# A sketched attention and an ELU block on one core: all large products in 128x64 tiles, boundary pieces last, and another order at a group's end

## The chip, the core and the metric

The kernel runs on one core of a Trainium2 chip. The core's engines run side by side, each with its own instruction queue that is worked in order: TensorE (PE) for products, VectorE (DVE), ScalarE (ACT), GpSimd (POOL), and SyncE (SP), which here only issues transfers. PE writes to PSUM, eight banks of 128 partitions x 512 fp32 numbers; the other operands lie in SBUF. The metric is the time of one execution on the device in microseconds (us), as the median of several runs.

## The reference

The first part is an attention without softmax (`q`, `k`, `v`: 4 batches, 4 heads, 1088 positions, head size 32; `S1`, `S2`: 8 x 32). The second is a two-layer block with ELU, on 4352 tokens of 128 features and 2048 hidden units.

```python
def phi(x):
    a = np.einsum('rd,bhsd->bhsr', S1, x)
    b = np.einsum('rd,bhsd->bhsr', S2, x)
    return np.einsum('bhsi,bhsj->bhsij', a, b).reshape(*x.shape[:-1], r * r)
q_p, k_p = phi(q), phi(k)
kv = np.einsum('bhsf,bhsd->bhfd', k_p, v)
z = np.sum(k_p, axis=2)
num = np.einsum('bhsf,bhfd->bhsd', q_p, kv)
den = np.einsum('bhsf,bhf->bhs', q_p, z)[..., None] + 1e-06
x = (num / den) laid out as (4352, 128)
h = x @ w_in
g = np.where(h > 0, h, np.exp(np.minimum(h, 0)) - 1)
out = g @ w_out
```

## The kernel before

**Tokens and groups.** The 4352 tokens are 68 half tiles of 64, 17 for each batch. Eight of them make a group `g` of 512 tokens; there are nine groups, 0 to 8, and the last has only 256. In groups 0 and 1 the second product is computed plainly. In groups 2 to 7 (`seven(g)`) it is computed with seven products in place of eight, from 2x2 blocks of the operands (the scheme of Winograd). Group 8 computes it with the operands swapped, so that tokens come out on partitions.

**The loop.** The hidden units are taken 256 at a time, in eight pairs `cp`. A step `n` of the list `steps` is one group and one pair. Lines 919 to 946 write the order of the work out by hand; each engine works through its own part of it in that order:
- `mm1` (line 696): two products of `W`'s columns with the group's tokens `xg`, into two PSUM banks `h` (four exist). Groups 2 to 7 do each as two halves of 64 columns (line 706, tile 128x64), the others as one (line 702, tile 128x128). The very first is `mm1_first` (line 714).
- `elu` for each of the two halves `c`: ScalarE runs a RELU of -h (line 723) and an exponential (line 725), VectorE joins them (line 731, result `gg`).
- in groups 2 to 7, `sums7` (lines 644 to 649): four sums `tt` of blocks of `gg` on GpSimd, one behind the first half, three behind the second.
- the second product of the step two before: `mm2` (line 744, 128x128), `mm2_seven` (line 664, fourteen halves of 128 moving columns in 128x64, accumulated in two banks `pa` and `pb`) or `mm2_last` (line 767, 128x128).

After a group's last step, `fin_seven` (line 669) copies three of the seven sums from `pa` on ScalarE (672), adds them up with what is in `pb` in five operations on VectorE (676 to 680), turns the result (682) and sends it out (693). `pa` and `pb` are single buffers: the next group's first products into them wait until they have been read. In a group's first step the products into `pa` come ahead of those into `pb`.

**Attention between the steps.** The dictionary `extra` puts pieces of the attention at chosen steps, in three places: behind `mm1` (`at`), between the two halves of the ELU (`mid`) and behind the second half (`late`). `KF_late` (309) projects `k`, `KA` (359) sums `kv` and, with `z_tile` (350), `z`; `turn` (lines 863 to 865) brings both to the other layout: `Z` (377), a product with 32 moving columns, and `KV` (391), two transposes on PE. `queries` (605) runs `q5` (589) of one unit around `q1` (493) of the next: `q5` for f = 0, then `q1`, then `q5` for f = 1. A unit is one group or, from group 4 on, two. Both functions use 16 tiles of 32x32, one for each head `h` and part `c` of the unit. Where a part straddles two batches, `parts(g, c)` gives two pieces, since each batch has its own operands, and the loops issue them one behind the other on the same tile. Units 2, 4 and 6 have one such part each. `q5_out` (603) and `q1_out` (505) take the results out, on ScalarE and VectorE.

Before 23.75 us the weights of the first pairs are rounded on VectorE (lines 99 to 125, `RA`, `RC`) and the first group's features are built; `Z_first` uses `Z` there too.

Of the kernel before, what the change touches and what calls it, by code (L numbers as in the profile page):

```python
# [12 lines left out]
F32 = mybir.dt.float32  # L13
# [14 lines left out]
def kernel(  # L28
# [184 lines left out]

    idle = psum.tile([P, 512], F32, name="idle", tag="o0", bufs=1)

    def keep_warm(n, cols=256):
        for i in range(n):
            nc.tensor.matmul(idle[:, :cols], some[:, :P], some[:, :cols], skip_group_check=True)  # L218
# [155 lines left out]

    def Z(b, ps, zl):

        nc.tensor.matmul(ps[:, 96:128], SXh[:], zl[:])

    def Z_out(b, ps):
        z = wzs[b] = SW[:, :, 2, :] if b == 0 else work.tile([FD, H, R], F32, name="wz", tag="wz")[:]  # L380
# [7 lines left out]

    def KV(b, ps):
        for f in range(2):  # L390
            nc.tensor.transpose(ps[:, 128 + P * f:128 + P * f + P], kvz[b][:, f].rearrange("p c s -> p (c s)"), ident[:])

    def KV_out(b, ps):
        nc.vector.tensor_copy(kvq[:, b].rearrange("p f h d -> p (f h d)"), ps[:, 128:384])
# [91 lines left out]


    def q1(g, ps, start=True):
        for c in range(4):
            for h in range(H):  # L490
                r = slice(D * h, D * h + D)
                for b, t, k, m in parts(g, c):
                    nc.tensor.matmul(ps[h][32 * c:32 * c + 32, 256 + 64 * k:256 + 64 * (k + m)],  # L493
                                     SWq[r, b].rearrange("p x r -> p (x r)"),
                                     qT[b][r, t:t + m, :].rearrange("p t s -> p (t s)"), start=start, stop=True,
                                     skip_group_check=True, tile_position=(D * h, 32 * c))
        abw[g] = ps

    def q1_out(g):
# [81 lines left out]

    def q5(g, ps, f):
        n = un[g]
        for h in range(H):
            i, o = divmod(h, heads(g))
            for c in range(4):
                r = slice(32 * c, 32 * c + 32)
                for j, (b, t, k, m) in enumerate(parts(g, c)):
                    nc.tensor.matmul(ps[c][D * h:D * h + D, 64 * k:64 * (k + m)], kvq[r, b, f, h, :],  # L589
                                     qpT[g, i][r, n * o + 2 * k:n * o + 2 * (k + m), f, :],  # L590
                                     start=(f == 0 and j == 0), stop=(f == 1),
                                     skip_group_check=True, tile_position=(32 * c, D * h))
        xps[g] = ps

    def q5_out(g, i=0):
# [28 lines left out]
    def seven(g):  # L624
        return 2 <= g < NQ - 1

    SS = const.tile([P, 4, NP, 64], F32, name="SS")
    ts, acc = {}, {}

    def weights7():  # L630
        a11, a21, a12, a22 = (W[:, :, 2 * P + 64 * i:2 * P + 64 * i + 64] for i in range(4))
# [19 lines left out]
    def mm2_seven(g, cp, first, last):  # L651
        if first:
            acc[g] = [psum.tile([P, 512], F32, name="pa", tag="o0", bufs=1),
                      psum.tile([P, 512], F32, name="pb", tag="o1", bufs=1)]
        a, b = acc[g]
        t, w = ts.pop((g, cp)), [W[:, cp, 2 * P + 64 * i:2 * P + 64 * i + 64] for i in range(4)]
        b11, b21, b22 = quarter(g, cp, 0, 0), quarter(g, cp, 1, 0), quarter(g, cp, 1, 1)
        p1, p2, p6 = (a, 0, w[0], b11), (a, 1, w[2], b21), (a, 2, SS[:, 1, cp], t[:, 1])
        p4, p5 = (b, 0, w[3], t[:, 3]), (b, 1, SS[:, 0, cp], t[:, 0])
        p7, p3 = (b, 2, SS[:, 2, cp], t[:, 2]), (b, 3, SS[:, 3, cp], b22)  # L660
        todo = [p1, p2, p6, p3, p5, p7, p4] if first else [p1, p2, p3, p5, p7, p6, p4]
        for i, (bank, col, lhs, rhs) in enumerate(todo):
            for u in range(2):
                nc.tensor.matmul(bank[64 * u:64 * u + 64, P * col:P * col + P], lhs, rhs[:, u],  # L664
                                 start=(first and i in (0, 3)), stop=last, skip_group_check=True,
                                 tile_position=(0, 64 * u))
        del gs[g, cp]

    def fin_seven(g):
        a, b = acc.pop(g)  # L670
        sa = work.tile([P, 3, P], F32, name="sa", tag="sa", bufs=1)
        nc.scalar.copy(sa[:].rearrange("p k s -> p (k s)"), a[:, :3 * P])
        pb = b[:].rearrange("p (k s) -> p k s", s=P)
        uu = work.tile([P, 3, P], F32, name="uu", tag="uu", bufs=1)
        cc = work.tile([P, 4, P], F32, name="cc", tag="cc", bufs=1)
        nc.vector.tensor_tensor(uu[:, 0], sa[:, 0], sa[:, 2], op=ADD)
        nc.vector.tensor_tensor(uu[:, 1:], _ap(uu[:, 0], [[0, 2], [1, P]]), pb[:, 1:3], op=ADD)
        nc.vector.tensor_tensor(cc[:, 2:], _ap(uu[:, 2], [[0, 2], [1, P]]), pb[:, 0:2], op=ADD)
        nc.vector.tensor_tensor(cc[:, 1], uu[:, 1], pb[:, 3], op=ADD)
        nc.vector.tensor_tensor(cc[:, 0], sa[:, 0], sa[:, 1], op=ADD)  # L680
        ob = work.tile([P, 2, 4, 2, D], F32, name="ob7", tag="ob", bufs=2)
        nc.vector.transpose(ob[:].rearrange("p h k w d -> p (h k w d)"), cc[:].rearrange("p k s -> p (k s)"))
        rows = out.rearrange("(b w y t) (e l d) -> b w e l y t d", b=B, w=2, t=NT, e=2, l=2)
        for u in range(2):
            k = 0
            while k < 4:
                bt, t = half_tile(g, 4 * u + k)
                m = min(4 - k, NT - t)
                for lo in range(2):
                    r = slice(64 * u + 32 * lo, 64 * u + 32 * lo + 32)  # L690
                    for hi in range(2):
                        for w in range(2):
                            nc.sync.dma_start(rows[bt, w, hi, lo, :, t:t + m, :], ob[r, hi, k:k + m, w, :])
                k += m

    def mm1(g, cp, cs=(0, 1)):
        n = qn[g] * P
        if 0 in cs and (g, cp) not in hs:
            hs[g, cp] = [psum.tile([P, 512], F32, name="h", tag="h", bufs=4) for c in range(2)]
        for c in cs:  # L700
            if not seven(g):
                nc.tensor.matmul(hs[g, cp][c][:, :n], W[:, cp, c * P:c * P + P], xg[g][:, :n])  # L702
                continue
            for u in range(2):
                r = slice(64 * u, 64 * u + 64)
                nc.tensor.matmul(hs[g, cp][c][r, :n], W[:, cp, c * P + 64 * u:c * P + 64 * u + 64], xg[g][:, :n],  # L706
                                 skip_group_check=True, tile_position=(0, 64 * u))

    def mm1_first():
        hs[0, 0] = [psum.tile([P, 512], F32, name="h", tag="h", bufs=4) for c in range(2)]  # L710
        for w in range(2):
            for c in range(2):
                cols = [x[:].rearrange("p (m w s) -> p w m s", w=2, s=P)[:, w] for x in (hs[0, 0][c], xg[0])]
                nc.tensor.matmul(cols[0], W[:, 0, c * P:c * P + P], cols[1], skip_group_check=True)

    def elu_a(g, cp, c, parts=(0, 1)):

# [20 lines left out]
    def mm2(g, cp, first, last):  # L738
        n = qn[g] * P
        if first:  # L740
            ops[g] = psum.tile([P, 512], F32, name="o", tag=f"o{g % 2}", bufs=1)
        gg = gs.pop((g, cp))
        for c in range(2):
            nc.tensor.matmul(ops[g][:, :n], W[:, cp, (2 + c) * P:(3 + c) * P], gg[:, c, :n],  # L744
                             start=(first and c == 0), stop=(last and c == 1))

    def fin1(g):
        n = qn[g] * P
# [11 lines left out]
    def mm2_last(cp, first, last):  # L760
        g = NQ - 1
        if first:
            ops[g] = [psum.tile([P, P], F32, name="ol", tag=t, bufs=k) for t, k in (("o0", 1), ("aux", 2))]
        gg = gs.pop((g, cp))
        for a in range(4):
            c, i = (a % 2, a // 2) if last else divmod(a, 2)
            nc.tensor.matmul(ops[g][i][:], gg[:, c, i * P:i * P + P], W[:, cp, (2 + c) * P:(3 + c) * P],  # L767
                             start=(first and c == 0), stop=(last and c == 1))

    def fin_last():  # L770
        g, n = NQ - 1, qn[NQ - 1]
# [147 lines left out]
    for n in range(2, N + 2):  # L919
# [5 lines left out]
        if n < N:  # L925
            elu(g, cp, 0)
            if seven(g):
                sums7(g, cp, 0)
            for f, *a in extra.get((n, 0), ()):
                f(*a)  # L930
            elu(g, cp, 1)
            if seven(g):
                sums7(g, cp, 1)
        for f, *a in extra.get((n, 1), ()):
            f(*a)
        g, cp = steps[n - 2]
        if g == NQ - 1:
            mm2_last(cp, cp == 0, cp == NP - 1)
        elif seven(g):
            mm2_seven(g, cp, cp == 0, cp == NP - 1)  # L940
            if cp == NP - 1:
                fin_seven(g)
        elif n > 2:
            mm2(g, cp, cp == 0, cp == NP - 1)
            if cp == NP - 1:
                fin1(g)
# [30 lines left out]
```

## Time and profile before

| what | us |
|---|---|
| median of 11 runs (272.60 to 274.82) | 274.35 |
| the profiled execution | 274.23 |
| its span | 272.4 |
| PE busy | 266.2 |
| VectorE busy | 190.8 |
| ScalarE busy | 183.4 |
| GpSimd busy | 166.2 |
| line 706, 384 records, mean 0.593 | 91.4 |
| line 744, 64 records, mean 0.604 | 30.8 |
| line 702, 92 records, mean 0.521 | 36.6 |

TensorE's granted clock is 0.999 of the full one. The times of PE's records [...] overlap: what a block costs is the distance from its start to the next block's start. Each fp32 product leaves two records, a transpose one. A timeline shows the start, the duration, the engine, the line, the operation, what is written from what, the tile (rows x columns of the array that an instruction uses), the moving shape and the number of records that were merged. A bracket at the end of a line names the idle time ahead of it and what ended it.

### The profile page before, as it was taken

What the parts mean: (1) busy time and instruction counts of PE and PEld (TensorE: products, weight loads), DVE (VectorE), ACT (ScalarE), POOL (GpSimd) and SP (SyncE); (2) the same over time, 40 slices, a digit from 0 to 9 for tenths busy, and PEclk for the clock granted to TensorE, in tenths of its full rate; (3) what the DMA queues carried; (4) which work ended last, traced back from release to release, by engine and by line L of the source; (5) the groups of instructions that cost most, each with busy time, mean ns of one, the idle gap of its engine ahead of it and who ended that gap; (6) DMA issues with size and microseconds to landing.
All of it is one profiled execution on the core that took longest, in us unless ns stands there. A gap on an engine that the chain in (4) does not pass through costs nothing.

```text
span 272.4 us, 7609 instructions
## 1 busy us (share of the span) xinstructions
PE 266.2 (98%) x3083; PEld 167.5 (61%) x3083; DVE 190.8 (70%) x350; ACT 183.4 (67%) x351; POOL 166.2 (61%) x233
## 2 busy tenths in 40 slices
PE   8899999999999999999999999999999999999994
PEld 5864444454442766666676666666766666667894
DVE  6699999997959796998648767564447444774552
ACT  2379978676564565776567677777677667777682
POOL 4500007204307985699969999989588988897200
PEclk9999999999999999999999999999999999999999
DMA  6996970011002200001100110001000200110021
GB/s 192 317 344 185 260 215 10 0 43 44 0 2 39 45 1 2 2 3 17 26 5 0 17 25 2 0 12 26 7 1 14 30 0 4 15 21 7 2 29 29
DMA packets 26418, 13.60 MB, mean 50 GB/s; under 512 B 19216, under 2 KB 24592, under 8 KB 26384
## 3 DMA queue, kind: packets, MB, share of 16 engines
q1 hardware_dynamic: 25792, 12.66, 18.8%
q8 instruction: 24, 0.39, 0.6%
q10 hardware_dynamic: 592, 0.46, 0.5%
q14 instruction: 10, 0.08, 0.1%
HBM read 10.88 MB, written 2.23 MB: 48 GB/s over the span
## 4 chain that ended last, share of the span: by engine, by line
PE 94%; DVE 4%; issue 1%; ACT 0%; DVEq 0%
PE h L706 30%; PE pb L664 16%; PE pa L664 12%; PE h L702 12%; PE o L744 11%; PE ol L767 3%; PE h L589 2%; PE idle L218 2%; PE kv L359 1%; PE abp L290 1%; PE qps L589 1%; DVE qp L536 1%; PE kfps L309 1%; PE h L493 1%; PE qps L493 1%
## 5 line engine op out<-in xcount | busy, mean ns | idle before, releaser
L731 DVE SCALAR_TENSOR_TENSOR gg<-e,h 128x512 f32<-128x512 f32 (+1 forms) x144 | 91.9, 652 | 64.7 <-ACT e L725 61.6
L723 ACT ACTIVATE e<-h 128x512 f32<-128x512 f32 (+1 forms) x144 | 81.6, 566 | 57.8 <-PE h L706 45.4
L706 PE MATMUL h<-xg,W 128*64 128x512 f32 x384 | 91.4, 593 | 0.0
L725 ACT ACTIVATE e<-e 128x512 f32<-128x512 f32 (+1 forms) x144 | 87.4, 607 | 4.6
L644 POOL TENSOR_TENSOR tt<-gg 128x256 f32<-128x256 f32 x48 | 36.3, 756 | 17.2 <-DVE gg L731 16.8
L706 PEld LDWEIGHTS h<-xg,W 128*64 128x64 f32 x384 | 27.9, 137 | 28.2 <-issue 24.9
L647 POOL TENSOR_TENSOR tt<-gg 128x256 f32<-128x256 f32 x48 | 38.3, 797 | 11.2 <-DVE gg L731 11.0
L649 POOL TENSOR_TENSOR tt<-gg,tt 128x256 f32<-128x256 f32 x48 | 37.7, 785 | 3.8
L648 POOL TENSOR_TENSOR tt<-tt,gg 128x256 f32<-128x256 f32 x48 | 37.0, 771 | 3.8
L664 PEld LDWEIGHTS pa<-gg,W 128*64 128x64 f32 x384 | 24.6, 137 | 22.4 <-issue 22.2
L702 PE MATMUL h<-xg,W 128*128 128x512 f32 (+1 forms) x92 | 36.6, 521 | 0.0
L744 PE MATMUL o<-gg,W 128*128 128x512 f32 x64 | 30.8, 604 | 0.4 <-DVE W L125 0.4
L664 PE MATMUL pa<-gg,W 128*64 128x128 f32 x384 | 30.3, 275 | 0.0
L664 PE MATMUL pb<-tt,SS 128*64 128x128 f32 x384 | 29.9, 273 | 0.0
L702 PEld LDWEIGHTS h<-xg,W 128*128 128x128 f32 x92 | 16.8, 190 | 14.9 <-issue 10.0
L664 PEld LDWEIGHTS pb<-tt,SS 128*64 128x64 f32 x384 | 23.3, 137 | 0.0
L744 PEld LDWEIGHTS o<-gg,W 128*128 128x128 f32 x64 | 11.4, 189 | 14.1 <-issue 11.9
L664 PE MATMUL pb<-gg,SS 128*64 128x128 f32 x192 | 19.5, 274 | 0.2
L664 PE MATMUL pb<-tt,W 128*64 128x128 f32 x192 | 19.4, 273 | 0.0
L664 PE MATMUL pa<-tt,SS 128*64 128x128 f32 x192 | 19.3, 273 | 0.0
L122 POOL TENSOR_TENSOR raw<-raw,tiny 128x512 f32<-128x512 f32 x1 | 1.0, 1046 | 29.3 <-DVE raw L117 29.3
L664 PEld LDWEIGHTS pb<-gg,SS 128*64 128x64 f32 x192 | 12.6, 137 | 1.0 <-issue 0.7
(141 smaller groups left out, 293.6 us busy)
## 6 DMA issues: line engine op xcount, KB each, us to landing
raw<-in_moe_w_in_dram SPq DMA_DIRECT2D x8, 256.0 KB, 5.9
raw<-in_moe_w_out_dram SPq DMA_DIRECT2D x8, 256.0 KB, 6.3
hd_k<-in_k_dram SPq DMA_DIRECT2D x3, 544.0 KB, 8.1
hd_q<-in_q_dram SPq DMA_DIRECT2D x3, 544.0 KB, 3.4
v<-in_v_dram SPq DMA_DIRECT2D x4, 288.0 KB, 6.8
out_dram<-ob SPq DMA_DIRECT2D x72, 16.0 KB, 1.5
v<-in_v_dram SPq DMA_DIRECT2D x4, 256.0 KB, 8.5
out_dram<-ob SPq DMA_DIRECT2D x16, 32.0 KB, 1.7
```

Source lines behind the costliest of these rows:

```text
L589: nc.tensor.matmul(ps[c][D * h:D * h + D, 64 * k:64 * (k + m)], kvq[r, b, f, h, :], qpT[g, i][r, n * o + 2 * k:n * o + 2 * (k + m), f, :], ...
L644: nc.gpsimd.tensor_tensor(t[:, 0], b12, b11, op=SUB)
L647: nc.gpsimd.tensor_tensor(t[:, 2], b22, b12, op=SUB)
L648: nc.gpsimd.tensor_tensor(t[:, 1], t[:, 2], b11, op=ADD)
L649: nc.gpsimd.tensor_tensor(t[:, 3], b21, t[:, 1], op=SUB)
L664: nc.tensor.matmul(bank[64 * u:64 * u + 64, P * col:P * col + P], lhs, rhs[:, u], start=(first and i in (0, 3)), stop=last, skip_group_che ...
L702: nc.tensor.matmul(hs[g, cp][c][:, :n], W[:, cp, c * P:c * P + P], xg[g][:, :n])
L706: nc.tensor.matmul(hs[g, cp][c][r, :n], W[:, cp, c * P + 64 * u:c * P + 64 * u + 64], xg[g][:, :n], skip_group_check=True, tile_position=( ...
L723: nc.scalar.activation(e, hs[g, cp][c][:, :n], RELU, scale=-1.0)
L725: nc.scalar.activation(e, e, EXP, scale=-1.0)
L731: nc.vector.scalar_tensor_tensor(gs[g, cp][:, c, :n], es[g, cp][:, c, :n], -1.0, hs[g, cp][c][:, :n], op0=ADD, op1=MAX)
L744: nc.tensor.matmul(ops[g][:, :n], W[:, cp, (2 + c) * P:(3 + c) * P], gg[:, c, :n], start=(first and c == 0), stop=(last and c == 1))
```

## The change

A new helper issues a product as two products of 64 columns each, in the two column tiles 128x64. It is used for the z product, the turning of kv (plain products with the identity in place of transposes), all first products, and the second products of groups 0, 1 and 8. In `q1` and `q5`, all first pieces are issued ahead of the second pieces. At a group's last step the order on ScalarE and VectorE is another: the products of `mm2_seven` are placed ahead of the second half's exponential in the written order (on PE they come behind the same work as before), the three products into `pa` come first, ScalarE copies only two of them between the RELU and the exponential of the second half, VectorE adds those up with the third, which it reads from PSUM, ahead of the second half of the ELU, and the rest follows behind it.

```diff
+    def halves(dst, lhs, rhs, **kw):
+        for u in range(2):
+            nc.tensor.matmul(dst[64 * u:64 * u + 64], lhs[:, 64 * u:64 * u + 64], rhs, skip_group_check=True,
+                             tile_position=(0, 64 * u), **kw)
...
-        nc.tensor.matmul(ps[:, 96:128], SXh[:], zl[:])
+        halves(ps[:, 96:128], SXh[:], zl[:])
...
-            nc.tensor.transpose(ps[:, 128 + P * f:128 + P * f + P], kvz[b][:, f].rearrange("p c s -> p (c s)"), ident[:])
+            halves(ps[:, 128 + P * f:128 + P * f + P], kvz[b][:, f].rearrange("p c s -> p (c s)"), ident[:])
...
+        todo = [(j, c, h, x) for c in range(4) for h in range(H) for j, x in enumerate(parts(g, c))]
+        for j, c, h, (b, t, k, m) in sorted(todo, key=lambda x: x[0]):
...
-                                     qT[b][r, t:t + m, :].rearrange("p t s -> p (t s)"), start=start, stop=True,
+                             qT[b][r, t:t + m, :].rearrange("p t s -> p (t s)"), start=start and j == 0, stop=True,
...
+        todo = [(j, h, c, x) for h in range(H) for c in range(4) for j, x in enumerate(parts(g, c))]
+        for j, h, c, (b, t, k, m) in sorted(todo, key=lambda x: x[0]):
...
-        todo = [p1, p2, p6, p3, p5, p7, p4] if first else [p1, p2, p3, p5, p7, p6, p4]
+        todo = [p1, p2, p6, p3, p5, p7, p4] if first or last else [p1, p2, p3, p5, p7, p6, p4]
...
+    def fin_seven_copy(g):
+        a = acc[g][0]
+        sa = sas[g] = work.tile([P, 2, P], F32, name="sa", tag="sa", bufs=1)
+        nc.scalar.copy(sa[:].rearrange("p k s -> p (k s)"), a[:, P:3 * P])
+
+    def fin_seven_a(g):
+        a, sa = acc[g][0], sas.pop(g)
...
+        nc.vector.tensor_tensor(uu[:, 0], sa[:, 1], a[:, :P], op=ADD)
+        nc.vector.tensor_tensor(cc[:, 0], sa[:, 0], a[:, :P], op=ADD)
+
+    def fin_seven_b(g):
...
         nc.vector.tensor_tensor(uu[:, 1:], _ap(uu[:, 0], [[0, 2], [1, P]]), pb[:, 1:3], op=ADD)
         nc.vector.tensor_tensor(cc[:, 2:], _ap(uu[:, 2], [[0, 2], [1, P]]), pb[:, 0:2], op=ADD)
         nc.vector.tensor_tensor(cc[:, 1], uu[:, 1], pb[:, 3], op=ADD)
-        nc.vector.tensor_tensor(cc[:, 0], sa[:, 0], sa[:, 1], op=ADD)
...
-            if not seven(g):
-                nc.tensor.matmul(hs[g, cp][c][:, :n], W[:, cp, c * P:c * P + P], xg[g][:, :n])
+            halves(hs[g, cp][c][:, :n], W[:, cp, c * P:c * P + P], xg[g][:, :n])
...
-                nc.tensor.matmul(cols[0], W[:, 0, c * P:c * P + P], cols[1], skip_group_check=True)
+                halves(cols[0], W[:, 0, c * P:c * P + P], cols[1])
...
-            nc.tensor.matmul(ops[g][:, :n], W[:, cp, (2 + c) * P:(3 + c) * P], gg[:, c, :n],
+            halves(ops[g][:, :n], W[:, cp, (2 + c) * P:(3 + c) * P], gg[:, c, :n],
...
-            nc.tensor.matmul(ops[g][i][:], gg[:, c, i * P:i * P + P], W[:, cp, (2 + c) * P:(3 + c) * P],
+            halves(ops[g][i][:], gg[:, c, i * P:i * P + P], W[:, cp, (2 + c) * P:(3 + c) * P],
...
-            elu(g, cp, 1)
+            before = steps[n - 2]
+            ends = n > 3 and seven(before[0]) and before[1] == NP - 1
+            if ends:
+                elu_a(g, cp, 1, (0,))
+                mm2_seven(*before, False, True)
+                fin_seven_copy(before[0])
+                elu_a(g, cp, 1, (1,))
+                fin_seven_a(before[0])
+                elu_d(g, cp, 1)
+            else:
+                elu(g, cp, 1)
             if seven(g):
                 sums7(g, cp, 1)
+            if ends:
+                fin_seven_b(before[0])
```

More of the change, by code (lines that the diff above doesn't have):

```diff
@@ L488, in q1 @@
     def q1(g, ps, start=True):
[L489 to L494, printed above, removed]
-                                     qT[b][r, t:t + m, :].rearrange("p t s -> p (t s)"), start=start, stop=True,
-                                     skip_group_check=True, tile_position=(D * h, 32 * c))
+        todo = [(j, c, h, x) for c in range(4) for h in range(H) for j, x in enumerate(parts(g, c))]
+        for j, c, h, (b, t, k, m) in sorted(todo, key=lambda x: x[0]):
+            r = slice(D * h, D * h + D)
+            nc.tensor.matmul(ps[h][32 * c:32 * c + 32, 256 + 64 * k:256 + 64 * (k + m)],
+                             SWq[r, b].rearrange("p x r -> p (x r)"),
+                             qT[b][r, t:t + m, :].rearrange("p t s -> p (t s)"), start=start and j == 0, stop=True,
+                             skip_group_check=True, tile_position=(D * h, 32 * c))
         abw[g] = ps
@@ L583, in q5 @@
         n = un[g]
-        for h in range(H):
+        todo = [(j, h, c, x) for h in range(H) for c in range(4) for j, x in enumerate(parts(g, c))]
+        for j, h, c, (b, t, k, m) in sorted(todo, key=lambda x: x[0]):
             i, o = divmod(h, heads(g))
[L586 to L592, printed above, removed]
+            r = slice(32 * c, 32 * c + 32)
+            nc.tensor.matmul(ps[c][D * h:D * h + D, 64 * k:64 * (k + m)], kvq[r, b, f, h, :],
+                             qpT[g, i][r, n * o + 2 * k:n * o + 2 * (k + m), f, :],
+                             start=(f == 0 and j == 0), stop=(f == 1),
+                             skip_group_check=True, tile_position=(32 * c, D * h))
         xps[g] = ps
@@ L627 @@
     SS = const.tile([P, 4, NP, 64], F32, name="SS")
-    ts, acc = {}, {}
+    ts, acc, sas = {}, {}, {}
     def weights7():
@@ L667, in mm2_seven @@
         del gs[g, cp]
[L669 to L673, printed above, removed]
+    def fin_seven_copy(g):
[4 more added lines that the diff above has]
+        a, sa = acc[g][0], sas.pop(g)
         uu = work.tile([P, 3, P], F32, name="uu", tag="uu", bufs=1)
         cc = work.tile([P, 4, P], F32, name="cc", tag="cc", bufs=1)
-        nc.vector.tensor_tensor(uu[:, 0], sa[:, 0], sa[:, 2], op=ADD)
+        sas[g] = uu, cc
+        nc.vector.tensor_tensor(uu[:, 0], sa[:, 1], a[:, :P], op=ADD)
+        nc.vector.tensor_tensor(cc[:, 0], sa[:, 0], a[:, :P], op=ADD)
+    def fin_seven_b(g):
+        b = acc.pop(g)[1]
+        uu, cc = sas.pop(g)
+        pb = b[:].rearrange("p (k s) -> p k s", s=P)
         nc.vector.tensor_tensor(uu[:, 1:], _ap(uu[:, 0], [[0, 2], [1, P]]), pb[:, 1:3], op=ADD)
@@ L700, in mm1 @@
         for c in cs:
-            if not seven(g):
[L702 to L707, printed above, removed]
+            halves(hs[g, cp][c][:, :n], W[:, cp, c * P:c * P + P], xg[g][:, :n])
     def mm1_first():
@@ L743, in mm2 @@
         for c in range(2):
-            nc.tensor.matmul(ops[g][:, :n], W[:, cp, (2 + c) * P:(3 + c) * P], gg[:, c, :n],
-                             start=(first and c == 0), stop=(last and c == 1))
+            halves(ops[g][:, :n], W[:, cp, (2 + c) * P:(3 + c) * P], gg[:, c, :n],
+                   start=(first and c == 0), stop=(last and c == 1))
     def fin1(g):
@@ L766, in mm2_last @@
             c, i = (a % 2, a // 2) if last else divmod(a, 2)
-            nc.tensor.matmul(ops[g][i][:], gg[:, c, i * P:i * P + P], W[:, cp, (2 + c) * P:(3 + c) * P],
-                             start=(first and c == 0), stop=(last and c == 1))
+            halves(ops[g][i][:], gg[:, c, i * P:i * P + P], W[:, cp, (2 + c) * P:(3 + c) * P],
+                   start=(first and c == 0), stop=(last and c == 1))
     def fin_last():
@@ L939 @@
         elif seven(g):
-            mm2_seven(g, cp, cp == 0, cp == NP - 1)
-            if cp == NP - 1:
-                fin_seven(g)
+            if cp < NP - 1:
+                mm2_seven(g, cp, cp == 0, False)
         elif n > 2:
```

## The prediction

> **What bounds the kernel now.** I read four views in this order: the chain that ended last, the timeline of TensorE (PE), the timeline of all engines at the end of one group, and the busy times by stretch. The chain, by engine:
>
> ```profile
> PE 94%; DVE 4%; issue 1%; ACT 0%; DVEq 0%
> ```
>
> PE carries nearly all of it. The DVE part lies before 23.75 us, where VectorE rounds weights and builds the first features; from 23.75 us on the end is set by the sum of PE's blocks. So I read the timeline of PE by the distance from one start to the next (the second column is modelled and runs past the next start). [...]
>
> ```profile
> 30.72 1.88 PE L702 MATMUL h<-xg,W 128*128 128x512 f32 x4
> 32.44 1.88 PE L744 MATMUL o<-gg,W 128*128 128x512 f32 x4
> ```
>
> Two products of 128x512 take 1.72 us in the 128x128 tile. In a stretch of pure 128x64 tiles (170.47, 172.00, 173.72 us) four half products of line 706 take 1.72 too, and the 14 halves of line 664 take 1.53, that is 0.2186 for a pair. Now the stretch where both kinds alternate:
>
> ```profile
> 78.19 1.94 PE L706 MATMUL h<-xg,W 128*64 128x512 f32 x8
> 80.06 0.72 PE L309 MATMUL kfps<-kT,Sxp 64*32 64x288 f32 x16
> 80.71 1.98 PE L744 MATMUL o<-gg,W 128*128 128x512 f32 x4
> 82.62 1.94 PE L706 MATMUL h<-xg,W 128*64 128x512 f32 x8
> 84.49 1.98 PE L744 MATMUL o<-gg,W 128*128 128x512 f32 x4
> ```
>
> The same work takes 1.91 (80.71 to 82.62) and 1.87. A block that enters 128x128 from another tile size costs about 0.10 more (also 58.97: 1.82), one that enters 128x64 about 0.05 (93.65: 1.58 for 1.53), and the block ahead of any change about 0.09 (37.59: 1.81 for 1.72). The last token group shows it again, with 256 moving columns:
>
> ```profile
> 250.87 1.13 PE L702 MATMUL h<-xg,W 128*128 128x256 f32 x4
> 251.93 0.66 PE L664 MATMUL pa<-gg,W 128*64 128x128 f32 x8
> ...
> 253.61 1.13 PE L702 MATMUL h<-xg,W 128*128 128x256 f32 x4
> ```
>
> 1.06 for line 702, where 258.20 to 259.07, with no change of tile, is 0.87; line 664's step is 1.68.
>
> **Part one: everything in 128x64.** Step by step, on PE's path:
> - 76.28 to 88.27, six blocks: 1.91 becomes 1.77 (still entered from 32x32 or 64x32) twice, 1.87 becomes 1.81, 1.72 and 1.81, 1.92 becomes 1.72. Gain 0.14+0.14+0.06+0.15+0.20+0.05 = 0.74.
> - Blocks of line 744 at 40.04, 58.97 and 67.21: entry at 0.05 in place of 0.10, gain 0.16.
> - 249.24 to 257.31: 1.63, 1.06, 1.68, 1.06, 1.68, 0.96 become 1.53, 0.87, 1.53, 0.87, 1.53, 0.87. Gain 0.87.
> - The eight steps of line 767: 0.89 becomes four pairs at 0.2186 = 0.875, gain 0.12.
> - Turning of z and kv. The two transposes at 47.02 take 0.21 (one record each); as plain products in halves they are two pairs of 128 columns, 0.44: a loss of 0.23. At 62.51, z and kv together take 0.39; after, 0.12 (z, my choice between 0.07 and 0.20; nearest row 0.14) + 0.44: a loss of 0.17. At 97.05 and 127.81 they stand between 128x64 blocks: 1.82+0.24+0.35+1.58 = 3.99 becomes 1.72+0.12+0.44+1.53 = 3.81, gain 0.18 each.
>
> Sum: 0.74+0.16+0.87+0.12-0.40+0.36 = 1.85 us. The first products (17.34 to 20.89) shed about 0.1 at their entry and pay it before the transposes of line 548; PE waits for VectorE at 23.75 anyway, so nothing is counted.
>
> A rule speaks against this. The Trainium skill, TensorEngine Tiling (Array Packing), section Instruction Overhead, gives each matmul about 60 cycles of overhead on trn2. Some 126 products are added by halving (34 of line 702 in the first two groups, lines 714 included, 16 in the last, 64 of lines 744 and 767, 12 of the turning). At 2.4 GHz, the clock that the skill's page Trainium Kernel Development and Optimization gives TensorE under NeuronCore Architecture, 60 cycles are 25 ns, an estimate: 3.15 us, more than this part gains. The rows decide: line 706 with twice the products keeps 1.72 us, so the price is nil at 512 columns, and line 664 shows 0.2186 a pair at 128, where line 767 whole takes 0.2225. I take nil.
>
> **Part two: boundary pieces last.** Only three units straddle a batch, each in one of four parts, so 4 extra products a set. Sets of 16 concurrent 32x32 tiles, with 128 moving columns:
>
> ```profile
> 74.28 0.61 PE L589 MATMUL h<-qpT,kvq 32*32 32x64 f32 x5
> ...
> 75.07 0.31 PE L493 MATMUL h<-qT,SWq 32*32 32x128 f32 x2
> ...
> 104.28 0.30 PE L589 MATMUL h<-qpT,kvq 32*32 32x128 f32 x2
> ...
> 104.60 0.42 PE L493 MATMUL h<-qT,SWq 32*32 32x128 f32 x3
> ```
>
> With a boundary the first set takes 0.79, without 0.32: an excess of 0.47, because the second piece has the first one's tile and holds up all behind it in order. For 256 columns I add 0.21, the step in mean duration being about 0.11 for 128 columns and two records a product: without a boundary 0.53, measured 0.69 twice (135.04, 190.22); last sets 1.03 against 1.22 twice, and 0.82 against 0.81 for the first unit; line 493's sets 0.40+0.21 = 0.61 against 0.78 and 0.70, and about 0.05 at 66.43. Excess in all: 0.47+0.32+0.37+0.17+0.09+0.05 = 1.47. Behind 15 other products, the first piece is done when the second comes (0.24 us of issue). But the pieces now stand just ahead of the next set's first tiles. Bounds -0.3 (every wait reappears, 9 sets) and 1.5; I take 1.1, near the upper end, since a tile's whole work is then no more than its neighbours'.
>
> **Part three: a group's last half products.** One group end, first VectorE (230.47: line 731 on its second half, ending the step), then PE:
>
> ```profile
> 231.07 0.28 DVE L676 TENSOR_TENSOR uu<-sa 128x128 f32<-128x128 f32 x1
> 231.46 0.42 DVE L677 TENSOR_TENSOR uu<-uu,pb 128x256 f32<-128x256 f32 x1
> 231.92 0.42 DVE L678 TENSOR_TENSOR cc<-uu,pb 128x256 f32<-128x256 f32 x1
> 232.26 0.28 DVE L679 TENSOR_TENSOR cc<-uu,pb 128x128 f32<-128x128 f32 x1
> ```
>
> ```profile
> 232.33 0.42 PE L664 MATMUL pa<-tt,SS 128*64 128x128 f32 x4
> 232.68 0.44 PE L664 MATMUL pb<-gg,SS 128*64 128x128 f32 x4
> ```
>
> The next group's first product into bank pb waits for line 679, the bank's last reader; it could start at 232.55, one pair behind the line above, and starts at 232.68. PE's order from step to step isn't changed. ScalarE now runs the RELU of the second half at 229.19, its exponential at 229.80 and the copy of 384 columns at 230.34. After, it copies 256 columns (about 0.34) ahead of the exponential: a new wait for three products. They are issued by 229.30, their results are there about 229.5, and the RELU ends at 229.77, so it doesn't stall. Behind it the exponential, then line 731's second half and GpSimd's sums slip 0.32; GpSimd idles 0.73 just after, and the sums are read two steps on, which hides it. VectorE puts two sums of 128 columns into its 0.40 of idling, then line 731 at 230.79 to 231.40, and lines 677, 678, 679 end the reads near 232.48, 0.06 sooner than 232.54. Three ends (176.96, 205.80, 231.89) are like this: 0.18. At 150.68, where line 572 occupies VectorE, the stall of 0.32 nearly vanishes: 0.30. At 119.47, with VectorE unbroken, it gets 0.06 worse; the wait for GpSimd at 117.49 stays, its product being last in both orders. Sum 0.42; bounds -0.4 (the delay is passed on) and 1.0 (all stalls behind 117.76 vanish).
>
> **Sum.** 1.85+1.1+0.42 = 3.4 us. The profiled execution took 274.23 (span 272.42 and 1.8 around it), so 270.85 of its own; the median shown is 274.35, so about 270.9. The eleven times lie in two clusters, 272.6 to 273.0 and 274.4 to 274.8, the profiled one in the upper; a median may land in either. A measurement of this kernel tells about 0.5% from no change: 1.4 us.
>
> **Rivals.**
> - Only the tile changes pay: the waits of parts two and three move but stay. For it: every piece still has to run before the next set's tile is free. Against it: 0.79 beside 0.32. It gives 274.35-1.85-0 = 272.5.
> - An engine behind PE takes over where PE quickens: VectorE is unbroken from 82.4 to 91.7 us, and ScalarE has 0.20 idle in steps of 1.76 in the last group. Against it: the result of 86.57 to 87.8 frees a bank that PE asks for at 90.50, and the last steps shrink by only 0.02. The price is the 0.74 of that stretch: 271.7.
> - Slower: a half product is not free where it replaces a whole one, because weight loads (137 ns for 64 columns) are no longer covered. The place is the 114 pairs of lines 702, 714, 744 and 767. At 25 ns each, 2.85, little is left: 273.8, no change. If one load showed in each, 114 x 0.137 = 15.6: 286.6. It turns the sign from 30 ns a pair. Against it stand the rows of lines 706 and 664, at the same shapes.
>
> **How the numbers follow.** My forecast, 270.9, has 0.60; tile changes alone, 272.5, 0.20; an engine behind, 271.7, 0.07; costly halves 0.13, of it 0.05 above 275.7. Faster by over 0.5% is the first three, less a tenth of the second: 0.85; within, 0.10; slower, 0.05. The range takes in the first three cases with the bounds of parts two and three, and part of the lower cluster: 269.2 to 272.9. All its main cases are of one sign.
>
> **What would show it.** Right: in the timeline after, all of 76 to 88 at 1.72 to 1.81 a block, the last group's steps at 0.87, 0.87 and 1.53, turning at 0.44, the first boundary set at 0.32 to 0.4, and pb following pa without a gap at 150.68. Wrong: blocks of lines 744 or 702 over 1.72 in halves; a set after the boundary pieces that starts later by what was saved; VectorE's chain at group ends longer; or PE waiting for e, gg or tt inside a step.

## The result, and the profile after

The changed kernel takes 270.68 us (median of 12 runs, 268.53 to 271.11), the kernel before 274.36 in the same measurements: a ratio of 0.9875, 95% interval 0.9851 to 0.9899. The forecast was 270.9. The times of each kernel lie in two clusters (last section), and both medians lie in the upper one. The profiled span fell from 272.4 to 268.6, by 3.8 us where the sum had 3.4.

Up to PE's first block of `mm2` (line 744, 23.75 us before) the profiled executions of all kernels below differ by up to 2.2 us, most of which does not come from the edits; the last section shows where it arises. Below, "the main stretch" is therefore the time from that block's start to the end of PE's last block: 23.75 to 268.94 before (245.19 us), 23.87 to 265.07 after (241.20): 3.99 us less. It is read from one execution of each kernel. Its blocks repeat well: between the kernel before and the two runs below that keep its tiles, all but the places named below agree within 0.03 us.

The chain by engine, after:

```profile
PE 88%; DVE 6%; POOL 2%; issue 1%; ACT 1%; DVEq 0%
```

PE still bounds; the chain goes over VectorE and GpSimd more often (6% and 2%), and one such place is found below. The same stretch of the timeline of PE as in the prediction (line 219 is the helper, x8 are two products as four halves):

```profile
78.10 1.89 PE L219 MATMUL h<-xg,W 128*64 128x512 f32 x8
79.92 0.71 PE L315 MATMUL kfps<-kT,Sxp 64*32 64x288 f32 x16
80.56 1.94 PE L219 MATMUL o<-gg,W 128*64 128x512 f32 x8
82.33 1.89 PE L219 MATMUL h<-xg,W 128*64 128x512 f32 x8
```

From start to start: 1.82 for the block that leaves for `KF_late`'s tile, 1.77 for the one that enters from it, and 1.72 for the last one shown, whose successor starts at 84.05. The last group's steps:

```profile
247.96 1.03 PE L219 MATMUL h<-xg,W 128*64 128x256 f32 x8
248.82 0.61 PE L668 MATMUL pa<-gg,W 128*64 128x128 f32 x8
...
250.35 1.03 PE L219 MATMUL h<-xg,W 128*64 128x256 f32 x8
```

0.86 and 1.53, where 1.06 and 1.68 stood. And the group end that the prediction worked out, the last reader of `pb` on VectorE and then PE:

```profile
229.34 0.28 DVE L692 TENSOR_TENSOR cc<-uu,pb 128x128 f32<-128x128 f32 x1
```

```profile
229.70 0.39 PE L668 MATMUL pa<-tt,SS 128*64 128x128 f32 x4
229.92 0.39 PE L668 MATMUL pb<-gg,SS 128*64 128x128 f32 x4
```

That reader ends at 229.62, 0.30 ahead of the first product into it; from `pa` to `pb` PE now takes 0.22, which is one pair.

Where the main stretch's 3.99 us came from, block by block in the two timelines: 76 to 89 us 0.74; the last group 0.90, its second products with the tail 0.16; turning at two places 0.19 and 0.18; small entries 0.10; less 0.28 for the stretches with the other two turnings, entries included: 1.99 for the tiles. The six blocks of query products became shorter by 0.20, 0.05, 0.22, 0.21, 0.63 and 0: 1.31. Group ends: 0.07+0.32+0.15+0.13+0.16, less 0.21 in the first end's first step: 0.62. Of that 0.21, 0.14 belongs to the order of the pieces, as the run with the pieces alone shows. Some hundredths are in no group.

### The profile page after: what moved, and what is told of

It reads as the page before. It is cut to its first block, busy times and chain, and to the rows that moved or that the text cites. A ratio compares the mean times of both kernels' runs of the same rounds, so it can differ in the third digit from the quotient of the medians.

```text
span 268.6 us, 8155 instructions
## 1 busy us (share of the span) xinstructions
PE 262.2 (98%) x3343; PEld 156.9 (58%) x3343; DVE 189.6 (71%) x350; ACT 182.1 (68%) x351; POOL 165.9 (62%) x233
## 4 chain that ended last, share of the span: by engine, by line
PE 88%; DVE 6%; POOL 2%; issue 1%; ACT 1%; DVEq 0%
PE h L219 40%; PE pb L668 15%; PE pa L668 12%; PE o L219 9%; PE ol L219 3%; PE h L593 2%; PE idle L224 2%; PE kv L365 1%; DVE gg L737 1%; DVE qp L541 1%; PE abp L296 1%; POOL kp L280 1%; PE kfps L315 1%; POOL tt L651 1%; PE kv L219 1%
## 5 line engine op out<-in xcount | busy, mean ns | idle before, releaser
L219 PE MATMUL h<-xg,W 128*64 128x512 f32 (+1 forms) x584 | 128.7, 563 | 0.0
L219 PEld LDWEIGHTS h<-xg,W 128*64 128x64 f32 x584 | 40.1, 137 | 47.4 <-issue 36.5
L652 POOL TENSOR_TENSOR tt<-tt,gg 128x256 f32<-128x256 f32 x48 | 36.0, 749 | 3.8
L668 PEld LDWEIGHTS pa<-gg,W 128*64 128x64 f32 x384 | 23.6, 137 | 22.6 <-issue 22.0
L219 PE MATMUL o<-gg,W 128*64 128x512 f32 x128 | 30.5, 597 | 0.4 <-DVE W L125 0.4
L668 PE MATMUL pa<-gg,W 128*64 128x128 f32 x384 | 29.5, 274 | 0.0
L668 PE MATMUL pb<-gg,SS 128*64 128x128 f32 x192 | 18.7, 273 | 0.0
L219 PEld LDWEIGHTS o<-gg,W 128*64 128x64 f32 x128 | 8.5, 136 | 15.8 <-issue 13.2
L668 PEld LDWEIGHTS pa<-tt,SS 128*64 128x64 f32 x192 | 12.1, 137 | 0.5 <-POOL tt L652 0.5
L668 PEld LDWEIGHTS pb<-tt,W 128*64 128x64 f32 x192 | 12.1, 137 | 0.0
```

What stands on the lines that cost most here:

```text
L219: nc.tensor.matmul(dst[64 * u:64 * u + 64], lhs[:, 64 * u:64 * u + 64], rhs, skip_group_check=True, tile_position=(0, 64 * u), **kw)
L652: nc.gpsimd.tensor_tensor(t[:, 1], t[:, 2], b11, op=ADD)
```

## The experiments

The theory was that the three parts add up, each with its size in the traces. The rival was that they need each other, an engine behind PE taking back what a part gives. Each part was put alone on the kernel before.

**The tiles alone** (`halves` everywhere; `q1`, `q5` and the group ends as before).

> The 128x64 tiles alone, pieces and group ends as before. Theory (three parts that add up, with the sizes that the two traces show block by block): the span falls by 2.0 us, from 272.4 to about 270.4; blocks from 76 to 88 us at 1.72 to 1.81, first boundary set at 74 us unchanged, stalls ahead of pb at the group ends still there. Rival (the parts need each other, since VectorE or ScalarE takes over when PE alone gets faster): under 1.2 us.

Measured: ratio 0.9922 (0.9891 to 0.9952); main stretch 243.01, that is 2.18 us less. Its span of 268.8 can't be compared with 272.4, since its main stretch happened to begin 1.5 us sooner. Against the expectation the block at 74 us did change, from 2.00 to 1.84: it holds a wait for VectorE, as a later run shows, and its length shifts with each edit ahead of it.

**The order of the pieces alone.**

```diff
-        for c in range(4):
-            for h in range(H):
...
-                for b, t, k, m in parts(g, c):
+        todo = [(j, c, h, x) for c in range(4) for h in range(H) for j, x in enumerate(parts(g, c))]
+        for j, c, h, (b, t, k, m) in sorted(todo, key=lambda x: x[0]):
```

> The order of the pieces alone. Theory: the six blocks of query products shorten by 0.20, 0.05, 0.22, 0.21, 0.63 and 0 us as between the two traces, the span by 1.3. Rival (those gains came from the tiles around the blocks, since entering and leaving is part of them): under 0.5.

Measured: ratio 0.9962 (0.9929 to 0.9995); main stretch 244.16, 1.03 less. The blocks take 0.58, 2.13, 1.70, 2.39, 1.90 and 0.79 (before: 0.78, 2.00, 1.92, 2.61, 2.54, 0.78). The gains of the theory are there but for the second block, which gets 0.13 longer: it gives back most of the first one's 0.20. A second place gives back most of the third one's 0.22. The step that ends the first group, 11 us behind that block, grows from 1.77 to 1.91, because PE now waits there for GpSimd's last sum:

```profile
117.75 0.44 PE L662 MATMUL pb<-tt,W 128*64 128x128 f32 x4 [0.16 <-POOL tt L647]
```

Counted from the start of the query block at 104 us, PE reaches this step after 11.48 in place of 11.71 us, but GpSimd's last two sums begin only 0.08 sooner. GpSimd's four sums run one behind the other and begin with a wait for VectorE, which in turn works without a break from 3.7 us behind the block's start on:

```profile
113.67 0.73 POOL L642 TENSOR_TENSOR tt<-gg 128x256 f32<-128x256 f32 x1 [2.03 <-DVE gg L729]
```

The step ends after 13.39 in place of 13.48 us, so 0.09 of the 0.22 is left. The six blocks add up to some 1.13; with this 0.14 off and some hundredths elsewhere, that is the 1.03.

**The order at a group's end alone** (`fin_seven` in its three pieces, the new place of `mm2_seven`, the new product order).

> The order at a group's end alone. Theory: the stalls ahead of pb vanish at four ends (0.32, 0.15, 0.13, 0.16), the first end gets 0.15 longer as a whole, the span falls by 0.6. Rival (the stalls vanished because the faster PE shifted the ends against VectorE's work): under 0.2.

Measured: ratio 0.9968 (0.9933 to 1.0003), which alone doesn't exclude no change; main stretch 244.36, 0.83 less. All four later ends start into `pb` without a stall; the first end takes 1.81 and 1.70 in its two steps, 3.51, where it was 3.53 before and not 0.15 longer as expected: the new order alone lengthens its first step by 0.04, not by the 0.21 seen in the changed kernel.

The three add up to 2.18+1.03+0.83 = 4.04, against 3.99 together. In sum the parts are independent within 0.05 us, and each lies above its rival's bound. Yet what the first rival names does happen at two places, the block at 74 us and the first group end, where VectorE and, through it, GpSimd take back 0.13 and 0.14 us of what the pieces give.

**The changes of tile put back.** To see whether the change of tile is the cause of the first part, and not halves that are cheaper in themselves:

```diff
-            halves(ops[g][:, :n], W[:, cp, (2 + c) * P:(3 + c) * P], gg[:, c, :n],
-                   start=(first and c == 0), stop=(last and c == 1))
+            nc.tensor.matmul(ops[g][:, :n], W[:, cp, (2 + c) * P:(3 + c) * P], gg[:, c, :n],
+                             start=(first and c == 0), stop=(last and c == 1))
```

> The changed kernel, with the second products of groups 0 and 1 (16 blocks) whole in 128x128 again, so that every step of these groups changes the tile twice. Theory (a change of tile costs 0.09 ahead of it and 0.05 or 0.10 behind it): ten blocks with both neighbours in 128x64 cost 0.33 each, six with one such neighbour 0.19: 4.4 us more than the changed kernel, a span of 273.0, beyond the kernel before. Rival (the saving comes from half products being cheaper in themselves, or from the waits between engines): at most 0.5 more.

Measured: ratio 1.0037 (1.0006 to 1.0068) to the kernel before; main stretch 245.86, 4.66 more than the changed kernel. Its timeline of PE:

```profile
84.01 1.98 PE L750 MATMUL o<-gg,W 128*128 128x512 f32 x4
85.92 1.94 PE L219 MATMUL h<-xg,W 128*64 128x512 f32 x8
87.79 1.98 PE L750 MATMUL o<-gg,W 128*128 128x512 f32 x4
```

1.91 and 1.87 again, wherever the two kinds alternate. The halves of line 219 are the same here as in the changed kernel, where they take 1.72, and cost 0.15 more between whole products: the change of tile is the cause. With enough of it the kernel is slower than before, by 0.67 us of main stretch.

**The two early sums put behind.**

```diff
                 elu_a(g, cp, 1, (1,))
+                elu_d(g, cp, 1)
                 fin_seven_a(before[0])
-                elu_d(g, cp, 1)
```

> The changed kernel, with the two sums that VectorE does ahead of the second half of the ELU put behind it; product order and early copy stay. Theory (VectorE's idling ahead of that half is what the sums fill): the last read of pb comes 0.35 us later at each end, a stall of 0.1 to 0.2 us at the usual ends and 0.3 to 0.4 where VectorE is unbroken: 0.8 to 1.0 us more than the changed kernel. Rival (the early copy and the product order are what removes the stall): no more than 0.2.

Measured: ratio 0.9888 (0.9848 to 0.9928); main stretch 242.62, 1.42 more than the changed kernel. The usual ends (groups 4 to 6) take 1.79 to 1.82, longer than before the change (1.66 to 1.69). One of them, VectorE and PE:

```profile
231.01 0.28 DVE L692 TENSOR_TENSOR cc<-uu,pb 128x128 f32<-128x128 f32 x1
```

```profile
230.95 0.42 PE L668 MATMUL pa<-tt,SS 128*64 128x128 f32 x4
231.44 0.44 PE L668 MATMUL pb<-gg,SS 128*64 128x128 f32 x4
```

PE waits until line 692 has read. So what removes the stall is the pair of sums in VectorE's idle time; the early copy and the product order without them make it longer. The ends of groups 2 to 6 account for some 1.1 of the 1.42: 0.27+0.28+0.26+0.29, and 0.02 at the first. A further 0.23 lies in the last 256-token steps (12.56 for 12.33 in the changed kernel). Of it, 0.17 is the end of group 7: the tile `ol` of `mm2_last` takes over the bank of `pa` (both have the tag `o0`), and its first product stands behind the second early sum, which reads `pa`:

```profile
254.90 0.28 DVE L684 TENSOR_TENSOR cc<-sa,pa 128x128 f32<-128x128 f32 x1
```

```profile
255.33 1.09 PE L219 MATMUL ol<-W,gg 128*64 128x128 f32 x16
```

The block ahead of `ol` takes 1.03 for 0.86 there.

**The gap in the block at 74 us.** In the changed kernel this block hardly shrank, and PE still stands still behind the first product of its first set:

```profile
74.38 0.67 PE L593 MATMUL h<-qpT,kvq 32*32 32x64 f32 x3
74.76 0.30 PE L593 MATMUL qps<-qpT,kvq 32*32 32x128 f32 x2
```

Its weight loads say why:

```profile
74.75 0.10 PEld L593 LDWEIGHTS h<-qpT,kvq 32*32 32x32 f32 x1 [0.24 <-DVE gg L737]
```

The third record belongs to another PSUM bank, and that bank is freed by the second half of an ELU. The test lengthens what stands ahead of that ELU:

```diff
     mid(14, q4, 2)
+    spare = const.tile([P, 512], F32, name="spare")
+    mid(14, nc.vector.memset, spare[:], 0.0)
```

> The changed kernel, with one more VectorE instruction (a fill of 128x512, about 0.3 to 0.6 us) ahead of the second half of the ELU in the step before the first unit's query products. Theory (the gap of 0.38 us behind the first product of that block is a wait for a PSUM bank that this ELU half frees, and not the boundary pieces): the gap grows by the whole duration of the fill. Rival (the gap is the two pieces on one tile): the gap stays at 0.38.

Measured in one execution:

```profile
74.48 0.48 DVE L938 MEMSET spare<- 128x512 f32 x1
```

```profile
75.56 0.10 PEld L593 LDWEIGHTS h<-qpT,kvq 32*32 32x32 f32 x1 [0.77 <-DVE gg L737]
```

The gap behind the first product grew from 0.37 to 0.90, by 0.53 where the fill takes 0.48, and the block from 1.95 to 2.48. It is a wait for VectorE. The kernel before has it as well: its block starts at 74.28, and the same half of the ELU ends at 74.48:

```profile
73.83 0.65 DVE L731 SCALAR_TENSOR_TENSOR gg<-e,h 128x512 f32<-128x512 f32 x1
```

**Transposes again for the turning of kv.**

```diff
-            halves(ps[:, 128 + P * f:128 + P * f + P], kvz[b][:, f].rearrange("p c s -> p (c s)"), ident[:])
+            nc.tensor.transpose(ps[:, 128 + P * f:128 + P * f + P], kvz[b][:, f].rearrange("p c s -> p (c s)"), ident[:])
```

> The changed kernel, with the turning of kv as two transposes in 128x128 again. Theory: 0.21 to 0.24 for the two, but a change of tile to and fro, 0.24 more, against 0.44 for the halves: within 0.05 at each of the four places, 0.2 us at most in all. Rival (the plain products cost 0.23 each time, as the first two places of the forecast had it): the span falls by 0.8 us.

Measured in one execution: main stretch 241.42, 0.22 more than the changed kernel; the rival falls. At the first place the two transposes take 0.37 where the halves take 0.44, but the blocks around them are 1.82 and 1.77 in place of 1.72: the change of tile eats the gain.

**A later transposition, and another product order at the ends.** What the change made worse is the first step of the first group end, 1.98 for 1.77. The pieces alone make it 1.91. The rest comes from the product order: the third product into `pa` is now one that needs GpSimd's third sum. This is its line in the changed kernel:

```profile
115.72 0.44 PE L668 MATMUL pa<-tt,SS 128*64 128x128 f32 x4 [0.23 <-POOL tt L652]
```

```diff
-        todo = [p1, p2, p6, p3, p5, p7, p4] if first or last else [p1, p2, p3, p5, p7, p6, p4]
+        todo = [p1, p2, p6, p3, p5, p7, p4] if first else [p1, p2, p3, p6, p5, p7, p4] if last else [p1, p2, p3, p5, p7, p6, p4]
...
-    late(24, transp, qT, "q", 3, 0, NT)
+    late(29, transp, qT, "q", 3, 0, NT)
```

> The changed kernel, with the last transposition of q (1.3 us on VectorE) moved from the step ahead of the first group end to one four steps later, and with the product that needs GpSimd's third sum fourth in place of third at a group's end. Theory: at the first group end the stall ahead of pb (0.16) vanishes and the wait for GpSimd shrinks from 0.45 to about 0.36, nothing else moves: 0.25 us less than the changed kernel, a span of 268.3. Rival (VectorE's late work is needed nowhere, so what moves only comes back at the later step): 0.

Measured: ratio 0.9834 (0.9794 to 0.9874); main stretch 241.02, 0.18 less than the changed kernel. The first end takes 1.92 and 1.53 for 1.98 and 1.69, and the step behind it has no stall:

```profile
117.15 0.39 PE L668 MATMUL pa<-tt,SS 128*64 128x128 f32 x4
117.37 0.39 PE L668 MATMUL pb<-gg,SS 128*64 128x128 f32 x4
```

The first step is back at what the pieces alone make it. One block of query products got 0.06 longer (2.46 for 2.40). The gain of 0.18 us over the changed kernel is shown by the timelines and not by the ratios: their intervals overlap, and three of the six executions here had the short start that the last section shows, against two of twelve of the changed kernel.

## Why the prediction was right

**Part one** held by its own steps. 76 to 88 us gave the 0.74 it had, the last group 0.90 for 0.87, the steps of line 767 with the tail 0.16 for 0.12, the two turnings between 128x64 blocks 0.18 each as said. The loss at the other two turnings came as worked out: 0.17 and 0.11 by their stretches, entries included, for 0.40 less the entries' 0.10. Putting the changes back cost 4.66 for an expected 4.4, so the prices of 0.09, 0.05 and 0.10 carry over. The rule of about 60 cycles a matmul, weighed as 3.15 us against this part, shows nowhere as an added price: halves keep 1.72 for 512 columns, and 256 columns take 0.86 where the whole product took 0.87.

**Part two** had the right sum by luck (1.1; measured 1.03 alone, 1.31 by the six blocks in the changed kernel) and wrong places. Its largest term, 0.47 at 74.28 for "the second piece has the first one's tile", failed: that gap is a wait for VectorE, and the block gave 0.05. The first set there, forecast at 0.32 to 0.4, takes 0.85, so one of the signs named for being right did not come. That the wait also swallows what the order gains ahead of it shows in the run with the pieces alone (2.13). The second mistake has the other sign: at 66 us the excess was 0.20, not 0.05, and the largest one was given nothing. At 190 us the first set still takes 0.69, but the set of line 493 behind it went from 0.63 to 0.31 and the last one from 1.22 to 0.91, together 0.63; the prediction gave no excess to the first of these. The sets that straddle a batch are not shorter themselves at 104 and 135 us either (0.78 to 0.81, 0.70 to 0.72); it is the set behind that runs in 0.57 for 0.82 and 0.99 for 1.22. The misses cancelled. What the sum left out is the first group end, which takes back 0.14.

**Part three** had the mechanism and sized one term wrongly. The copy occupies ScalarE for 0.25 in the queue, not 0.34, and follows the RELU after 0.47, not 0.58, since neighbours on an engine overlap by a part of their listed durations. So the second ELU half starts 1.93 us behind the step's first product, where 2.14 was worked out, and the last read of `pb` starts 0.29 sooner than before, not 0.06: the usual stalls vanish instead of shrinking to half. The "new wait" on the three products doesn't stall ScalarE at the usual ends, as said. At the first end the step "the wait for GpSimd at 117.49 stays, its product being last in both orders" held nearly for this part alone (1.81 for 1.77), although with the new order PE also waits for the third sum, now in the third product. It failed for the three parts together (1.98), and most of that is part two: PE comes 0.22 sooner behind the query block at 104 us, while the sums keep their place behind it. In all ten traces the step ends 13.39 to 13.52 us after that block's start, whether it takes 1.76 (the tiles alone) or 1.98.

The rival of an engine behind PE didn't show where it was expected, from 82 to 92 us and in the last group, but at the block at 74 us and at the first group end, where PE waits for `tt` inside a step, which was named as a sign of being wrong; the two are worth some 0.3 us. Costly halves are excluded by the rows, and the rival that only the tiles pay by the two single runs and by the timelines.

## What to carry to other kernels

Where one engine bounds, read the distance from one block's start to the next, and sort the blocks by what stands ahead of and behind them: equal work with unequal distance shows the price of a change of mode, which no busy time shows. When a set of small products starts late, look at its weight loads' wait before blaming the order of the products. The stall at the hand-over went away here when work was put into an idle gap that was already there; moving something early without that made it longer. And where a second engine works without a break for 10 us, a block that shrinks on the bounding engine can give its gain back at the next wait, far from the edit: look for it there.

## What the runs showed of the hardware

**A change of tile.** In one tile size, the weights of the next block are loaded one product ahead of it; where the tile changes, the first load starts only with the block. First the changed kernel (block from 84.05 us), then the kernel before (block from 84.49):

```profile
83.62 0.14 PEld L219 LDWEIGHTS o<-gg,W 128*64 128x64 f32 x2 [0.28 <-issue]
```

```profile
84.49 0.30 PEld L744 LDWEIGHTS o<-gg,W 128*128 128x128 f32 x2 [0.81 <-issue]
```

The block then starts 0.52 behind the last product ahead of it where neighbours of one tile have 0.43 between products, and its own second product follows the first after 0.53 in 128x128 and 0.48 in 128x64. These are the prices of 0.09, 0.10 and 0.05. That the late load is their cause fits its size (0.19 and 0.13 for one load), but no run tested it.

**The start.** The eleven times of the kernel before, and those of most others, lie in two clusters about 1.7 to 2 us apart. The profiled executions show a difference in the first 9 us. First the kernel before (profiled at 274.23, in the upper cluster), then the kernel with the tiles alone (270.60, in its lower one, 270.55 to 270.94; the upper is 272.18 to 272.82):

```profile
5.62 1.22 PE L218 MATMUL idle<-some 128*128 128x256 f32 x2
6.77 2.38 PE L290 MATMUL abp<-Sab,kT 128*64 128x64 f32 x33
```

```profile
5.11 0.70 PE L224 MATMUL idle<-some 128*128 128x256 f32 x2
5.74 1.67 PE L296 MATMUL abp<-Sab,kT 128*64 128x64 f32 x36
```

The same two records of filling work take 1.15 from start to start in the one and 0.63 in the other, near a factor of two, and the first large block starts at 23.75 or 22.26. The granted clock of the profile reads 1.00 in both up to there. It can show a halved clock: in the run with the fill it reads 0.50 from 12 to 14 us, and the main stretch starts at 23.72 although the filling work at 5 us ran at 0.63. Nor is the clock all: in the run with the changes of tile put back, VectorE gets the first part of `q` from its transfer 0.94 us later than with the tiles alone (7.67 for 6.73), and the main stretch begins 0.94 later. The Trainium skill, TensorE: Matmul & The Clock Gate, Part 1, describes a gate at half speed whose window runs free of the kernel's start, and warns that its recorded events aren't reliable; the two speeds fit that, but no run here changed it on purpose, so the cause is argued and not shown.
